# A chunked attention and feed-forward kernel: seven-product second layer from the third group of tokens on, its weight sums one group sooner

## The chip, the cores and the metric

The kernel runs on one core of a Trainium2 chip. Its time is in microseconds of the device, from the start to the end of one execution. A core has a matrix engine (TensorE, "PE" in the profile; its weight loads, "PEld", are listed apart), VectorE ("DVE"), ScalarE ("ACT"), GpSimd ("POOL") and SyncE ("SP"), which here issues nearly all transfers. The engines run their own instruction streams side by side and wait for one another by semaphores.

## The reference

```python
# q, k, v: (8, 8, 576, 64) fp32; w_in: (512, 2048), w_out: (2048, 512) fp32
q_c, k_c, v_c = (a.reshape(B, H, 9, 64, D) for a in (q, k, v))
scores = scale * np.matmul(q_c, k_c.transpose(0, 1, 2, 4, 3))     # scale = 1/8
scores = scores - np.max(scores, axis=-1, keepdims=True)
attn = np.exp(scores)
attn = attn / (np.sum(attn, axis=-1, keepdims=True) + 1e-09)
x = np.matmul(attn, v_c).reshape(B, H, S, D).transpose(0, 2, 1, 3).reshape(4608, 512)
h = x @ w_in
out = (h - np.tanh(h)) @ w_out
```

Attention is taken inside chunks of 64 tokens. Its result, 4608 tokens of 512, goes through a feed-forward net of two layers, with h − tanh(h) between them.

## The kernel before

**Tiles and groups.** The 4608 tokens are 36 tiles of 128, in nine groups of four (`SIZES`, L34), so 512 tokens a group. The hidden width of 2048 is cut into 16 units of 128, numbered fc. For each group and unit, the first layer makes the tile ph (128 hidden values by 512 tokens), ACT takes tanh of it, DVE subtracts (`shrink`, tile t), ACT rounds the result to a high half gh, DVE takes the low half gl = t − gh (`split`), and the second layer adds this unit's share to four output tiles po in PSUM. The second layer of a unit stands two units behind its first layer, and two ph tiles exist, so PE always has one layer to do while the others work on the unit between.

**Products of halves.** Every factor is held as a high and a low half, and a product is high x high, low x high and high x low, so three matmuls per block. In the plain form both layers of a unit take 3 x 4 = 12 matmuls of 128x512 (`gemm1`, L572, and `gemm2`, L601) on the 32-bit type F32R. From the third group (number 2) on the first layer uses 16-bit halves of the weights instead. In the fast form (`Fast`, L646) the unit is two 128-wide blocks of the hidden layer (j and j + 8) by two tiles of tokens, and the second layer is taken by seven products in place of eight, with sums and differences of blocks: 7 x 3 = 21 matmuls of 128x256 (L709). For it the weights need their own sums, once. `combine` (L499 to L523) makes them on POOL, five steps for each of eight j, and `shorten` (ACT L534, DVE L535) rounds four pieces of each to 16-bit halves. The activations need sums too, in each unit (POOL, L678 to L680).

**Weights.** They come as 64-bit words from two transfers a unit and are rebuilt on the chip: ACT L146, DVE L150, L151, L152 (shifts and masks that put the bits together), then the high half on ACT (`high`, L155) and the low half on DVE (`low`, L159). All of it lies in group 0. `square` (L110) gives ACT's sum of squares of a weight tile, from which powers of two for the 16-bit forms are made (`powers`, with `partition_all_reduce` on POOL). `convert` (L484 to L494) turns a first-layer weight tile into 16-bit halves: two operations on ACT (L490, L491), two on DVE (L493, L494).

**Which group does what, before.** Group 0 runs both layers in F32R. Its work follows `PLAN` (L55), a string of tokens; the part ahead of the bar is in exactly that order, the rest is placed by the scheduler. Group 1 too is F32R, from `run` (L603) with the scheduler's order; beside it lie the attention of group 2 (`interleaved`, L434), the squares of the second layer's weights and the 16 conversions. Group 2 has the 16-bit first layer, the second layer in F32R; it is written in a fixed order (`written`, L620, inside `manual_schedule`), and beside it lie the weight sums and their shortening, and attention of group 3. Groups 3 to 8 are the fast form, each beside the attention of the next group (`ahead`, L776). In the fixed order `at[k]` is a list of pieces that are issued at half step k: 2s after the first layer of the s-th unit, 2s + 1 after the second layer that follows it.

**Names.** wh and wl are the halves of a weight tile; a name like wl014 is layer 0, unit 14, and wh113 layer 1, unit 13. raw is a weight tile as loaded and w the rebuilt one. xh and xl are the halves of the token tiles, rawk and rawv the loaded keys and values of an attention, psa its PSUM tile, a and s its scores. gh and gl are the halves of the activations. place names that repeat a weight tile's name (wl11 as target of a sum) are other uses of the same memory.

Of the kernel before, what the change touches and what calls it, by code (L numbers as in the profile page):

```python
# [22 lines left out]
P = 128  # L23
H = 8
# [14 lines left out]
LAG = 2  # L39
FAST = 3  # L40
# [8 lines left out]


BASE = (3, 18)
LATER = (8, 20)
STEPS = (0, 1, 2, 3, 4, 5, 6, 11)
# [6 lines left out]
def attn_ffn_kernel(ctx: ExitStack, tc: tile.TileContext, qE, kE, vE, qL, kL, vL, w_in, w_out, out):  # L60
# [20 lines left out]
    wt, half_w, fast_w, w_pool = [[None, None] for _ in range(FC)], [None] * FC, {}, {}  # L81

# [29 lines left out]
    def power(pool, name, sums, to, back):  # L112


        n = sums.shape[1]
        top = pool.tile([P, n], F32, name=f"{name}top", bufs=2)
        nc.gpsimd.partition_all_reduce(top, sums, channels=P, reduce_op=bass_isa.ReduceOp.max)
        power_of_two(top, to, back)

# [5 lines left out]

    def largest(a, out):

        nc.vector.tensor_reduce(out=out, in_=a, axis=AX.X, op=ALU.max, apply_absolute_value=True)
        nc.vector.tensor_scalar_mul(out, out, 2.0 ** -12)
# [24 lines left out]
    def high(fc, part):  # L154
        nc.scalar.copy(out=wt[fc][part][0], in_=ws[fc][:, part].bitcast(F32))  # L155
# [118 lines left out]
    class Late:  # L274
# [4 lines left out]
        def __init__(self, pool):  # L279
            self.pool, self.st = pool, defaultdict(dict)  # L280

            self.raw = {n: xpool.tile([P, KC, MOST], F32R, name="xl").bitcast(F32) if n == "q" else pool.tile([P, MOST // P, H * CH], F32, name=f"raw{n}", bufs=1) for n in "qkv"}
            self.q16 = self.v16 = self.k16 = self.aT = self.junk = None

        def load(self, p, i):
            for n, src in (("q", qL), ("k", kL), ("v", vL)):
                nc.sync.dma_start(out=self.raw[n][:, i], in_=src[p - NE])

        def sums(self, g, n, other=None):
# [4 lines left out]
            some = self.raw[n][:, :SIZES[g]]  # L294
            if n != "v" and other is not None:
                spread(other.bitcast(U8).rearrange("p (a n) -> p a n", n=H * CH), some, d["sums"][:, "qkv".index(n):"qkv".index(n) + 1])
                return
            if n != "v":
                junk = self.pool.tile([P, 4, H * CH], F16, name="a", bufs=1).bitcast(U8).rearrange("p a n -> p (a n)")[:, :MOST * H * CH // P].rearrange("p (a n) -> p a n", n=H * CH) if self.junk is None else self.junk
                spread(junk, some, d["sums"][:, "qkv".index(n):"qkv".index(n) + 1])  # L300
                return
            largest(some.rearrange("p i n -> p (i n)"), d["sums"][:, 2:3])
            if other is None:
                self.scales(g)
# [10 lines left out]

        def scales(self, g):
            self.across(g)
            self.spread_out(g)
# [21 lines left out]
        def split(self, g, b, n):  # L340
# [4 lines left out]
            if n == "k":  # L345
                hl = self.k16
                if hl is None:
                    t = self.pool.tile([P, 2, 2 * H * CH], F16, name="a", bufs=1)
                    hl = t[:, 0], t[:, 1]
                d["k"] = hl  # L350
# [21 lines left out]
        def exponents(self, g, b):  # L372
            self.shifted(g, b)
            self.exponent(g, b)

# [11 lines left out]

        def normalise(self, g, b):
            self.totals(g, b)
            self.divided(g, b)  # L390
# [15 lines left out]
        def transpose(self, g, b):  # L406
# [5 lines left out]
            if self.aT:  # L412
                aT = self.aT
            else:
                t = self.pool.tile([P, 2, 4, 2, CH], F32, name="s", bufs=1).rearrange("p e hp c k -> p (e hp c k)").bitcast(F16)
                aT = [t[:, e * 2 * H * CH:(e + 1) * 2 * H * CH] for e in range(2)]
# [17 lines left out]
    def interleaved(att, g, x):  # L434

        at = defaultdict(list)
# [598 lines left out]
```

## Time and profile before

| What | us |
|---|---|
| Median of 3 runs | 820.54 |
| The runs | 818.73 to 821.04 |
| The profiled execution | 818.66 |
| Its span | 816.9 |
| PE busy | 803.5 |
| DVE busy | 644.5 |
| ACT busy | 467.4 |
| POOL busy | 381.1 |

The span is from the first to the last instruction; the profiled execution's own time is 1.8 us longer. Busy shares are averages over nine groups with different limits: group 0 has the weights to rebuild, groups 1 and 2 are single, groups 3 to 8 repeat. In a row of windows a stretch is given by its bounds in us, with the busy time of each engine and the number of its instructions. In the timeline a wait stands behind a row in brackets, with the instruction that ended it. Matmul rows overlap a little, since the next begins before the last has drained.

### The profile page before, as it was taken

The numbers are of one execution on the slowest core, as the hardware profiler recorded it, in microseconds if no ns is written. First come the engines' busy times: TensorE is split into PE (matmuls) and PEld (weight loads), VectorE is DVE, ScalarE is ACT, GpSimd is POOL, SyncE is SP. The second block draws the span as 40 slices with busy tenths as digits, with TensorE's granted clock in tenths as the row PEclk, the third lists the DMA queues.
The fourth block names the chain that finished last, engine by engine and source line by source line (L and its number), as shares of the span: only waits on it lengthen the run. The fifth ranks groups of instructions, "written<-read, shape, count | busy, mean of one in ns | idle before, by whom it ended". The sixth has DMA issues, their size and how long they took to land.

```text
span 816.9 us, 20560 instructions
## 1 busy us (share of the span) xinstructions
PE 803.5 (98%) x8805; PEld 664.6 (81%) x8805; DVE 644.5 (79%) x853; ACT 467.4 (57%) x754; POOL 381.1 (47%) x385
## 2 busy tenths in 40 slices
PE   8999999999999999999999999999999999999997
PEld 5677787788756568888888888888888888888886
DVE  6899986877459999797879787878887887877553
ACT  5698779665345457564745474546554655454332
POOL 2000000000028666856665756575666665757563
PEclk9999999999999999999999999999999999999999
DMA  7954523321201113122222322222222220202000
GB/s 250 344 180 156 187 86 140 105 53 34 71 1 30 49 37 120 27 79 53 80 53 79 53 79 53 79 53 79 52 80 52 79 53 2 53 3 52 2 27 26
DMA packets 58459, 63.19 MB, mean 77 GB/s; under 512 B 32768, under 2 KB 38912, under 8 KB 58368
## 3 DMA queue, kind: packets, MB, share of 16 engines
q1 hardware_dynamic: 57792, 61.10, 25.1%
q8 instruction: 69, 1.13, 0.6%
q10 hardware_dynamic: 576, 0.79, 0.3%
q14 instruction: 22, 0.18, 0.1%
HBM read 45.09 MB, written 9.44 MB: 67 GB/s over the span
## 4 chain that ended last, share of the span: by engine, by line
PE 80%; DVE 10%; ACT 5%; POOL 2%; issue 2%; DVEq 0%; ACTq 0%
PE ph L669 29%; PE po L709 26%; PE po L601 10%; PE ph L572 10%; PE psa L364 3%; PE ph L854 1%; DVE w L151 1%; DVE gl L592 1%; DVE w L152 1%; ACT wh L155 1%; ACT s L228 1%; ACT w L146 1%; ACT junk L110 1%; DVE wh L535 1%; PE psa L193 1%
## 5 line engine op out<-in xcount | busy, mean ns | idle before, releaser
L669 PE MATMUL ph<-xh,wl 128*128 128x256 f16 x2160 | 249.5, 273 | 0.0
L669 PEld LDWEIGHTS <-wl 128*128 128x128 f16 x2160 | 209.8, 98 | 25.2 <-issue 0.5
L678 POOL TENSOR_TENSOR xl<-xl 128x256 f32<-128x256 f32 x96 | 97.1, 1011 | 183.8 <-DVE xl L677 182.9
L676 ACT ACTIVATE t<-ph,sig 128x512 f32<-128x512 f32 x96 | 65.8, 685 | 147.6 <-PE ph L669 146.9
L677 DVE SCALAR_TENSOR_TENSOR xl<-ph,sig,t 128x512 f32<-128x512 f32 x96 | 71.6, 746 | 46.5 <-ACT t L676 46.3
L709 PEld LDWEIGHTS <-wh 128*128 128x128 f16 x1008 | 98.7, 98 | 11.4
L679 POOL TENSOR_TENSOR xl<-xl 128x128 f32<-128x128 f32 x96 | 105.5, 1099 | 0.0
L680 POOL TENSOR_TENSOR xl<-xl 128x256 f32<-128x256 f32 x96 | 93.1, 970 | 0.0
L709 PE MATMUL po<-wl,wh 128*128 128x256 f16 x576 | 89.7, 273 | 0.0
L690 DVE SCALAR_TENSOR_TENSOR wh<-xl,to_g,wh 128x896 f16<-128x896 f32 x48 | 64.6, 1346 | 30.0 <-ACT wh L689 30.0
L689 ACT ACTIVATE wh<-xl,to_g 128x896 f16<-128x896 f32 x48 | 49.9, 1039 | 60.8 <-POOL xl L680 60.8
L601 PE MATMUL po<-wh,gh 128*128 128x512 f32 x192 | 79.5, 414 | 1.0 <-ACT gh L591 0.8
L690 DVE SCALAR_TENSOR_TENSOR gl<-xl,to_g,gh 128x896 f16<-128x896 f32 x48 | 71.8, 1496 | 9.1 <-ACT gh L689 8.9
L601 PE MATMUL po<-wl,gh 128*128 128x512 f32 x192 | 75.7, 394 | 0.9 <-POOL wl L159 0.9
L572 PE MATMUL ph<-xh,wl 128*128 128x512 f16 (+2 forms) x316 | 76.5, 380 | 0.0
L601 PE MATMUL po<-wh,gl 128*128 128x512 f32 x192 | 75.1, 396 | 1.0 <-DVE gl L592 1.0
L709 PE MATMUL po<-wh,wh 128*128 128x256 f16 x432 | 75.9, 273 | 0.0
L709 PEld LDWEIGHTS <-gh 128*128 128x128 f16 x672 | 64.9, 98 | 7.8
L709 PE MATMUL po<-wh,gh 128*128 128x256 f16 x336 | 54.4, 273 | 0.0
L709 PE MATMUL po<-wl,gh 128*128 128x256 f16 x336 | 52.4, 273 | 0.0
L592 DVE TENSOR_TENSOR gl<-t,gh 128x512 fp32r<-128x512 f32 (+1 forms) x50 | 40.0, 800 | 15.5 <-ACT gh L591 15.3
L689 ACT ACTIVATE gh<-xl,to_g 128x896 f16<-128x896 f32 x48 | 49.5, 1032 | 4.2 <-POOL xl L680 4.1
(159 smaller groups left out, 1402.5 us busy)
## 6 DMA issues: line engine op xcount, KB each, us to landing
raw<-w_in SPq DMA_DIRECT2D x16, 512.0 KB, 3.7
raw<-w_out SPq DMA_DIRECT2D x16, 512.0 KB, 4.6
rawk<-kL SPq DMA_DIRECT2D x28, 256.0 KB, 3.9
rawv<-vL SPq DMA_DIRECT2D x28, 256.0 KB, 3.6
xl<-qL SPq DMA_DIRECT2D x28, 256.0 KB, 2.9
out<-wh SPq DMA_DIRECT2D x46, 128.0 KB, 1.8
q<-qE SPq DMA_DIRECT2D x8, 256.0 KB, 5.2
v<-vE SPq DMA_DIRECT2D x8, 256.0 KB, 4.5
```

The source lines that it names most:

```text
L572: nc.tensor.matmul(ph, lhsT=self.weight(fc, 0, a)[:, kc * P:(kc + 1) * P], rhs=x[b][:, kc, cols], start=(k == 0), stop=(k == 3 * KC - 1))
L592: nc.vector.tensor_sub(gl, t, gh)
L601: nc.tensor.matmul(self.po[t], lhsT=gg[a][:, ts], rhs=self.weight(fc, 1, b), start=(fc == 0 and i == 0), stop=(fc == FC - 1 and i == 2))
L669: nc.tensor.matmul(self.ph[:, 1 - f::2, :], lhsT=half_w[fc][:, w, kc * P:(kc + 1) * P], rhs=rhs, start=(k == 0), stop=(k == 3 * KC - 1))
L676: nc.scalar.activation(t, self.ph, AF.Tanh, scale=sig)
L677: nc.vector.scalar_tensor_tensor(out=u[:, :4], in0=self.ph, scalar=sig, in1=t, op0=ALU.mult, op1=ALU.subtract)
L678: nc.gpsimd.tensor_add(u[:, 4:6], u[:, 1:3], u[:, 0:4:3])
L679: nc.gpsimd.tensor_add(u[:, 6], u[:, 1], u[:, 2])
L680: nc.gpsimd.tensor_sub(u[:, 0:4:3], u[:, 0:2], u[:, 2:4])
L689: nc.scalar.activation(gh, u, AF.Copy, scale=powers[1])
L690: nc.vector.scalar_tensor_tensor(out=gl, in0=u, scalar=powers[1], in1=gh, op0=ALU.mult, op1=ALU.subtract)
L709: nc.tensor.matmul(place[m], lhsT=part[:, self.SUM[m]], rhs=w[m][:, o], start=first, stop=(last and part is gl), skip_group_check=True)
```

## The change

`FAST` goes from 3 to 2: the fast form, with its seven products, begins with the third group. For that, the weight sums and the 16-bit forms have to be there one group sooner.

- Group 1 is now written in a fixed order, over the units 0, 8, 1, 9 and so on (`ORDER`), as group 2 was. Beside it lie all that lay beside group 1 and group 2: powers of two, 16 conversions, sums of the second layer's weights for j from 0 to 5 and their shortening, and attention of group 2 (in place of that of group 3). The shortening of each j starts one step later than before, at 4j + 12 in place of 4j + 10; the sums start at the same half steps. The last two j follow at the start of group 2.
- `gemm2` in F32R takes for all four tiles first gh by wh and gh by wl, and then gl by wh for all four, in place of the three products tile by tile.
- The low half gl of the first four units of group 1 is made by POOL, the others by DVE.
- The high halves of first-layer weights of the units 8 to 15 (`SHORT`) are cut to 11 bits by a mask on DVE, into the memory of raw, before ACT copies them. With it the two DVE operations of `convert` are left out for these units.
- The measure of the second layer's weights is moved into group 0: for the first eight units squares on ACT, for the others (`SQUARED`) the largest absolute value by a reduction on DVE. `powers` is cut in two (`most`, with the reductions over the partitions, and `powers`).
- The loads for group 2's attention come as all of q, then k, then v.

```diff
-FAST = 3
+FAST = 2
+MASK = 0xFFFFE000
+SHORT = 8
+SQUARED = 8
+ORDER = tuple(i // 2 + i % 2 * FC // 2 for i in range(FC))
...
     def high(fc, part):
-        nc.scalar.copy(out=wt[fc][part][0], in_=ws[fc][:, part].bitcast(F32))
+        w = ws[fc][:, part]
+        if part == 0 and fc >= SHORT:
+
+            short = raws[fc][:, part].rearrange("p n a -> p (n a)")[:, :DM]
+            nc.vector.tensor_single_scalar(short, w, MASK, op=ALU.bitwise_and)
+            w = short
+        nc.scalar.copy(out=wt[fc][part][0], in_=w.bitcast(F32))
...
             nc.scalar.activation(l16, l, AF.Copy, scale=to)
+            if fc >= SHORT:
+                return
             rest = place_of("l", 0, fc)[:, :DM]
...
-    def split(self):
+    def split(self, engine=None):
...
-            nc.vector.tensor_sub(gl, t, gh)
+            (engine or nc.vector).tensor_sub(gl, t, gh)
...
-            for t in range(t0, t1):
-                ts = slice((t - t0) * P, (t - t0 + 1) * P)
-                for i, (a, b) in enumerate(((0, 0), (0, 1), (1, 0))):
-                    nc.tensor.matmul(self.po[t], lhsT=gg[a][:, ts], rhs=self.weight(fc, 1, b), start=(fc == 0 and i == 0), stop=(fc == FC - 1 and i == 2))
+            for some in ((0, 0), (0, 1)), ((1, 0),):
+                for t in range(t0, t1):
+                    ts = slice((t - t0) * P, (t - t0 + 1) * P)
+                    for a, b in some:
+                        nc.tensor.matmul(self.po[t], lhsT=gg[a][:, ts], rhs=wt[fc][1][b], start=(fc == 0 and a == b), stop=(fc == FC - 1 and a == 1))
...
             if self.ready:
-                self.split()
+                self.split(nc.gpsimd if s <= 4 else None)
...
     for fc in range(FC):
         square(fc, 0, junk)
+    for fc in range(SQUARED):
+        square(fc, 1, junk)
+    for fc in range(SQUARED, FC):
+        nc.vector.tensor_reduce(out=sums_w[1][:, fc:fc + 1], in_=wt[fc][1][0].bitcast(F32), axis=AX.X, op=ALU.max, apply_absolute_value=True)
...
+    at[0].append(loads)
+    at[1] += [lambda: half.most(0), lambda: half.most(1)]
+    at[4] += [lambda: half.powers(0), lambda: half.powers(1)]
+    for i, fc in enumerate(ORDER):
+        at[max(2 * i + 1, 5 + (3 * i + 1) // 2)].append(lambda i=i, fc=fc: half.convert(fc, place_of("l", 0, ORDER[i - 1]) if i else first_place))
...
     for j in range(FC // 2 - 2):
-        at[4 * j + 7].append(lambda j=j: make(j, 5))
+        at[4 * j + 7].append(lambda j=j: make(j, 5 if j else 4))
+        if j == 0:
+            at[11].append(lambda: make(0, 1))
         for i in range(4):
-            at[4 * j + 10 + i].append(lambda j=j, i=i: half.shorten(j, slice(i, i + 1)))
+            at[4 * j + 12 + i].append(lambda j=j, i=i: half.shorten(j, slice(i, i + 1)))
...
-        ff = FeedForward(FAST - 1, nx)
+        ff = FeedForward(1, nx)
...
-        for s in range(FC):
-            ff.written(s, s // 2 + s % 2 * FC // 2, at)
+        for s, fc in enumerate(ORDER):
+            ff.written(s, fc, at)
```

What this makes of the order is shown at three places. The first is DVE at the end of group 0, where the weights of the units 13 to 15 are rebuilt. Before, its rows were these (line, operation, target and sources, shape):

```order
L151 SCALAR_TENSOR_TENSOR w_1376<-raw_1373,w_1376 128x1024
L592 TENSOR_TENSOR gl_1358<-t_1354,gh_1357 128x512
L152 SCALAR_TENSOR_TENSOR w_1376<-raw_1373,w_1376 128x1024
L150 TENSOR_SCALAR w_1420<-w_1420 128x1024
L151 SCALAR_TENSOR_TENSOR w_1420<-raw_1417,w_1420 128x1024
L159 TENSOR_TENSOR wl014_1105<-w_1376,wh014_1104 128x512
L159 TENSOR_TENSOR wl114_1107<-w_1376,wh114_1106 128x512
```

Now, for the same unit 14 (its w is w_1382, its lines are some ten to fifteen lower):

```order
L847 TENSOR_REDUCE sums1_103<-wh112_1098 128x1
L137 SCALAR_TENSOR_TENSOR w_1382<-raw_1379,w_1382 128x1024
L136 TENSOR_SCALAR w_1427<-w_1427 128x1024
L138 SCALAR_TENSOR_TENSOR w_1382<-raw_1379,w_1382 128x1024
L527 TENSOR_TENSOR t_1405<-ph_1392,t_1405 128x512
L145 TENSOR_SCALAR raw_1379<-w_1382 128x512
L151 TENSOR_TENSOR wl114_1107<-w_1382,wh114_1106 128x512
L535 TENSOR_TENSOR gl_1409<-t_1405,gh_1408 128x512
L151 TENSOR_TENSOR wl014_1105<-w_1382,wh014_1104 128x512
```

A reduction (L847) and a mask (L145) stand between the operations of the unit, and its first-layer low half (wl014) now comes behind that of the second layer and behind a gl.

The second place is DVE in the middle of group 1. Before, between two subtractions t there stood a conversion (L493, L494) and at times a piece of attention (L354):

```order
L584 TENSOR_TENSOR t_2034<-ph_2021,t_2034 128x512
L354 SCALAR_TENSOR_TENSOR a_2235<-rawk_1543,to_1721,a_2235 128x1024
L592 TENSOR_TENSOR gl_2038<-t_2034,gh_2037 128x512
L493 SCALAR_TENSOR_TENSOR wl09_2197<-wh09_1084,to_w_1546,wl08_2194 128x512
L494 TENSOR_TENSOR wl08_2194<-wl08_2194,wl09_2197 128x512
L584 TENSOR_TENSOR t_2073<-ph_2060,t_2073 128x512
```

Now, in the eighth unit of the same group:

```order
L527 TENSOR_TENSOR t_1917<-ph_1904,t_1917 128x512
L447 SCALAR_TENSOR_TENSOR wl03_1923<-wh03_82,to_w_1570,wl010_1920 128x512
L448 TENSOR_TENSOR wl010_1920<-wl010_1920,wl03_1923 128x512
L330 SCALAR_TENSOR_TENSOR a_1926<-rawk_1567,to_1829,a_1926 128x1024
L489 SCALAR_TENSOR_TENSOR wh018_1839<-wh18_1741,to_w_1570,wh018_1839 128x512
L330 SCALAR_TENSOR_TENSOR wh09_1877<-rawv_1568,to_1829,wh01_1876 128x1024
L489 SCALAR_TENSOR_TENSOR wh02_1840<-wh10_1738,to_w_1570,wh02_1840 128x256
L535 TENSOR_TENSOR gl_1968<-t_1917,gh_1967 128x512
L527 TENSOR_TENSOR t_1984<-ph_1971,t_1984 128x512
```

Conversion, attention (L330) and two shortenings (L489) stand between one t and the gl that belongs to it.

The third place is PE, in the second layer of one unit of group 1. Before, the three products went tile by tile:

```order
L601 MATMUL po0_1568<-wh11_76,gh_1626 128x512
L601 MATMUL po0_1568<-wl11_77,gh_1626 128x512
L601 MATMUL po0_1568<-wh11_76,gl_1627 128x512
L601 MATMUL po1_1569<-wh11_76,gh_1626 128x512
L601 MATMUL po1_1569<-wl11_77,gh_1626 128x512
```

Now:

```order
L545 MATMUL po2_1577<-wl18_1083,gh_1645 128x512
L545 MATMUL po3_1578<-wh18_1082,gh_1645 128x512
L545 MATMUL po3_1578<-wl18_1083,gh_1645 128x512
L545 MATMUL po0_1575<-wh18_1082,gl_1646 128x512
L545 MATMUL po1_1576<-wh18_1082,gl_1646 128x512
```

The first matmul that reads gl moved from the third place of twelve to the ninth.

More of the change, by code (lines that the diff above doesn't have):

```diff
@@ L38 @@
 MOST = max(SIZES) * P
-LAG = 2
-FAST = 3
+FAST = 2
 FAST_LAG = 2
@@ L282, in __init__, with load, sums @@
             self.raw = {n: xpool.tile([P, KC, MOST], F32R, name="xl").bitcast(F32) if n == "q" else pool.tile([P, MOST // P, H * CH], F32, name=f"raw{n}", bufs=1) for n in "qkv"}
[L283 to L286 removed]
+            self.q16 = self.v16 = None
+        def load(self, p, i, some="qkv"):
+            for n in some:
+                src = {"q": qL, "k": kL, "v": vL}[n]
                 nc.sync.dma_start(out=self.raw[n][:, i], in_=src[p - NE])
[L289 removed]
+        def sums(self, g, n, other):
             d = self.st[f"g{g}"]
@@ L293, in sums @@
                 d["sums"] = self.pool.tile([P, 3], F32, name="sums", bufs=2)
[L294 to L304, printed above, removed]
+            spread(other.bitcast(U8).rearrange("p (a n) -> p a n", n=H * CH), self.raw[n], d["sums"][:, "qkv".index(n):"qkv".index(n) + 1])
         def halves(self, g, i):
@@ L411, in transpose @@
             nc.vector.tensor_sub(a[:, :, 1], s, a[:, :, 0])
[L412 to L416, printed above, removed]
+            t = self.pool.tile([P, 2, 4, 2, CH], F32, name="s", bufs=1).rearrange("p e hp c k -> p (e hp c k)").bitcast(F16)
+            aT = [t[:, e * 2 * H * CH:(e + 1) * 2 * H * CH] for e in range(2)]
             d["a16"] = []
@@ L553, in __init__ @@
             self.g, self.x, self.queue, self.po, self.ready = g, x, [], [], None
-            self.half = g > 1
-            if g > 1:
-                self.sig = half.power_of(g)[0]
-        def weight(self, fc, part, i):
-            return half_w[fc][:, i] if self.half and part == 0 else wt[fc][part][i]
         def room(self, pool, tiles):
@@ L571, in gemm1 @@
                 for kc in range(KC):
-                    nc.tensor.matmul(ph, lhsT=self.weight(fc, 0, a)[:, kc * P:(kc + 1) * P], rhs=x[b][:, kc, cols], start=(k == 0), stop=(k == 3 * KC - 1))
+                    nc.tensor.matmul(ph, lhsT=wt[fc][0][a][:, kc * P:(kc + 1) * P], rhs=x[b][:, kc, cols], start=(k == 0), stop=(k == 3 * KC - 1))
                     k += 1
@@ L781, in put @@
             at[o + 2 * unit + part].append(lambda: f(*args))
+        late = g == FAST
         for unit, n in (1, "q"), (2, "k"):
-            put(unit, 0, lambda n=n: att.sums(g, n, ffn.tile([P, MOST], F32, name="t", bufs=3)))
-        put(-3 if g > FAST else 1, 0, att.halves, g, 0)
-        put(2, 1, att.halves, g, 1)
+            put(unit + late, 0, lambda n=n: att.sums(g, n, ffn.tile([P, MOST], F32, name="t", bufs=3)))
+        put(3 if late else -3, 0, att.halves, g, 0)
+        put(3 if late else 2, 1, att.halves, g, 1)
         put(4, 1, att.across, g)
@@ L924, in attn_ffn_kernel, with loads @@
     late = ctx.enter_context(tc.tile_pool(name="att", bufs=1, side="right", reuse_waits="tile"))
+    w_pool.update((fc, late) for fc in SPARE)
     att, half = Late(late), Half(late)
[L926 to L929 removed]
+    xs, powers, at, made = {}, {}, defaultdict(list), {}
     first_place = late.tile([P, DM], F32, name="first_place", bufs=1).bitcast(F16)
[L931 to L957 removed]
+    def loads():
+        for n in "qkv":
+            for i in range(SIZES[FAST]):
+                att.load(FIRST[FAST] + i, i, n)
     def make(j, steps):
```

140 lines of the change are left out of this document (33 added, 107 removed).

## The prediction

> **What bounds the kernel now.** First the page: span, busy shares, and the chain that ended last, by engine.
>
> ```profile
> span 816.9 us, 20560 instructions
> PE 803.5 (98%) x8805; PEld 664.6 (81%) x8805; DVE 644.5 (79%) x853; ACT 467.4 (57%) x754; POOL 381.1 (47%) x385
> ...
> PE 80%; DVE 10%; ACT 5%; POOL 2%; issue 2%; DVEq 0%; ACTq 0%
> ```
>
> TensorE is busy for 98% of the span, so time is won by taking matmuls away and lost wherever another engine newly makes PE wait. Next the chain in order of time (start, us, engine, tile, line, count), from the end of group 0's weights to the first units of the seven-product groups.
>
> ```profile
> 92.28 2.35 DVE w L151 x2
> ...
> 168.33 2.76 PE ph L572 x12
> 171.09 2.80 PE po L601 x12
> ...
> 285.49 2.79 PE po L601 x12
> 288.28 2.60 PE ph L572 x12
> ...
> 354.19 2.62 PE ph L669 x24
> 356.81 2.29 PE po L709 x21
> ```
>
> Before 100 us the chain still runs through DVE (group 0's weights, L151); in the stages after it is PE. Then the windows of the stages touched (busy us of PE, PEld, DVE, ACT, POOL, granted clock, DMA share): the first has the stretch of group 2 in which the weight sums are shortened, then the end of group 0's weights, all of group 2, the start of group 3, and group 1.
>
> ```profile
> 247.30:300.40 53.10, 52.07 (x416) 32.32 (x415) 51.39 (x58) 26.48 (x41) 43.07 (x32) 1.00 0.15 41
> 100.00:120.00 20.00, 20.00 (x90) 16.57 (x89) 18.86 (x32) 14.51 (x31) 0.84 (x2) 1.00 0.34 110
> 220.80:305.30 84.50, 83.47 (x557) 51.32 (x557) 67.72 (x81) 42.62 (x65) 49.10 (x37) 1.00 0.12 37
> 311.10:350.90 39.80, 37.84 (x421) 32.76 (x423) 34.10 (x42) 25.49 (x34) 33.12 (x33) 1.00 0.25 68
> 128.00:220.80 92.80, 92.80 (x770) 74.66 (x768) 66.56 (x113) 59.33 (x96) 1.94 (x2) 1.00 0.21 61
> ```
>
> PE is full everywhere, at full clock. But DVE runs right behind it in two of the stages: 18.86 of 20 us at the end of group 0, and 51.39 of 53.10 us where the weight sums are made. Group 1 is easy: DVE 66.56 of 92.80, POOL idle. The change lays work on DVE in the first and moves the crowd of the second into group 1.
>
> **What is taken away.** Group 2's second layer goes from twelve 128x512 matmuls per unit to 21 of 128x256: 2.79 us (row 285.49) to 2.29 (356.81), 16 units: −8.0 us. Its first layer becomes 24 half-width matmuls, 2.62 against 2.60: +0.3. Sum **−7.7 us**, on PE, which sets the end there. Group 1's own matmuls stay as many (other order only).
>
> **The end of group 0.** On DVE come eight masks (L145 of the changed kernel, 128x512) and eight largest-value reductions (L847). The nearest rows of DVE's timeline (start, us of one or of x, line, tiles): a reduction over 128x512, a bit operation on 128x1024, the last weights, and two operations right behind each other.
>
> ```profile
> 70.01 0.68 DVE L237 TENSOR_REDUCE sm<-s 128x8 f32<-128x512 f32 x1
> ...
> 100.43 0.69 DVE L150 TENSOR_SCALAR w<-w 128x1024 uint32<-128x1024 uint32 x1
> ...
> 115.55 1.29 DVE L159 TENSOR_TENSOR wl<-w,wh 128x512 fp32r<-128x512 f32 x2
> ...
> 304.65 0.68 DVE L592 TENSOR_TENSOR gl<-t,gh 128x512 fp32r<-128x512 f32 x1
> 305.25 0.74 DVE L581 SCALAR_TENSOR_TENSOR t<-ph,sig,t 128x512 f32<-128x512 f32 x1
> ```
>
> PE's timeline: the first layer of group 0's last unit, and its last wait there.
>
> ```profile
> 118.51 1.07 PE L572 MATMUL ph<-xh,wh 128*128 128x512 f32 x4
> 119.41 1.07 PE L572 MATMUL ph<-xh,wl 128*128 128x512 f32 x4
> ...
> 124.82 0.50 PE L601 MATMUL po<-wh,gh 128*128 128x512 f32 x1 [0.23 <-ACT gh L591]
> ```
>
> An operation of 0.68 holds the engine for about 0.60 (rows 304.65 and 305.25: the next starts 0.60 later). A mask of half the row at 100.43 is so worth 0.33, and 8 x 0.33 = 2.6; six of the eight reductions stand ahead of the last low half by the order of the changed kernel, 6 x 0.60 = 3.6. Together 6.2 us of new work on an engine with 1.1 idle in 20. The cover: the last low weight half is done at 116.84, PE first uses it at 119.41, 2.6 later. In the new order three second-layer matmuls of 0.23 stand ahead of that first layer, and the wait of 0.23 at 124.82 can go, together about 1.0. So 6.2 − 2.6 − 1.0 = **+2.5 us**, rounded; the ends are 0 (DVE's idle time and ACT, rid of half the squares in group 1, take it) and 6.2 (no cover).
>
> **Group 1 as the crowded stage.** What squeezed group 2 was shortening on DVE beside POOL's sums. Groups by form in group 2's stage (busy, mean ns of one, idle before):
>
> ```profile
> L592 DVE TENSOR_TENSOR gl<-t,gh 128x512 fp32r<-128x512 f32 x15 | 17.0, 1132 | 3.1 <-ACT gh L591 3.1
> ...
> L535 DVE SCALAR_TENSOR_TENSOR wl<-wh,to_w,wl 128x512 f16<-128x512 f32 x10 | 9.6, 960 | 0.0
> ```
>
> All this now stands in group 1, and with it part of the conversion of the first layer's weights, which used to lie in group 1 alone. The groups there:
>
> ```profile
> L493 DVE SCALAR_TENSOR_TENSOR wl<-wh,to_w,wl 128x512 f16<-128x512 f32 x15 | 11.2, 748 | 4.8 <-PE ph L572 3.4 <-ACT wl L491 1.4
> ...
> L494 DVE TENSOR_TENSOR wl<-wl,wl 128x512 f16<-128x512 f16 x15 | 6.3, 422 | 0.3
> ```
>
> The conversions of the masked eight need no DVE any more. Of the other eight, five fall into the steps in which sums are shortened, two shortenings a step as before. Alone they cost 5 x (0.748 + 0.422) = 5.9 us; stretched like the shortenings, which are operations of the same kind (0.960 against 0.748, 1.28 times), 7.5; stretched like gl (1.132 against 0.68, 1.66 times), 9.7. Ten steps of group 1 (2.76 + 2.80 = 5.56 against 2.79 + 2.60 = 5.39) are 1.7 longer. So DVE has 4.2 to 8.0 us more to do than that stage allowed before; by the kind that is nearest, 5.8.
>
> How far may it fall behind? ACT's tanh, and rows of PE's timeline: the only wait on gl, the last unit's first layer, and the wait after the stage.
>
> ```profile
> 303.83 0.69 ACT L580 ACTIVATE t<-ph,sig 128x512 f32<-128x512 f32 x1
> ```
>
> ```profile
> 280.32 0.50 PE L601 MATMUL po<-wh,gl 128*128 128x512 f32 x1 [1.03 <-DVE gl L592]
> ...
> 299.89 2.76 PE L572 MATMUL ph<-xh,wl 128*128 128x512 f16 x12
> 302.31 0.58 PE L601 MATMUL po<-wh,gh 128*128 128x512 f32 x1
> ...
> 350.86 0.94 PE L364 MATMUL psa<-a,wh 64*64 64x64 f16 x92 [1.94 <-DVE a L354]
> ```
>
> There are two ph buffers: the first layer of unit n+2 begins two units after that of unit n began, 2 x 5.39, and that of unit n itself takes 302.31 − 299.89 = 2.42 up to the next matmul. In the 8.36 between must lie tanh (0.69) and the subtraction (0.74): 6.9 us are left. The last unit's products end at 302.65 (299.89 + 2.76), tanh could be done 0.69 later, and DVE starts the subtraction at 305.25: it was 1.9 behind at the end of the stage. That leaves 5.0. The low half gl is now first needed by the ninth matmul of a unit instead of the third, 6 x 0.23 = 1.4 later: 6.4 in reserve against 5.8, so on balance nothing is lost. But the wait of 1.03 at 280.32 came with the reserve far from used up: single low halves stand behind a bunch of attention work. The new stage has two bunches with conversions in them, steps 7 and 8 and step 14. I give each the middle of the two waits that DVE's bunches caused before (1.03 and 1.94), 1.5, and take off the 1.03 of the stage that is replaced: **+2.0 us**. The ends: −1.0, all covered, since the first four units' low halves go to POOL (idle there: 1.94 of 92.80) and the ninth matmul waits less; and 8.0, if no lag can be carried. I take 2.0, because it comes from waits on the same engine in the stage most like it. I count on the lag carried out of the stage being made up in the next one, where DVE has 39.80 − 34.10 = 5.7 us free.
>
> At nothing go: POOL's gl, about 1.4 us each (the POOL rows below) with more than one whole first layer, 2.76, before it is needed, which would cost its length if that cover went; the two reductions over the partitions and the small powers, early in group 1 where DVE has 28% free; the loads of group 2 in another order, at least two steps ahead of their use; the mask's ACT cast, which is as long as before.
>
> **The sum.** −7.7 + 2.5 + 2.0 = −3.2 us. The profiled run took 818.66 us (span 816.9), 1.88 below the median of the runs, 820.54. So 815.5 in that run and **817.3** against the median.
>
> [...] Beside POOL the same subtraction differs widely; a row of DVE's timeline, then two of POOL's from the same stretch:
>
> ```profile
> 257.13 1.78 DVE L592 TENSOR_TENSOR gl<-t,gh 128x512 fp32r<-128x512 f32 x1
> ```
>
> ```profile
> 257.00 1.36 POOL L509 TENSOR_TENSOR wh<-wh,wl 128x512 f32<-128x512 f32 x1
> 258.44 1.61 POOL L512 TENSOR_TENSOR wl<-wh,wh 128x512 f32<-128x512 f32 x1
> ```
>
> 1.78 us beside POOL and 0.68 alone (304.65): the mean of 1.13 in this stage is a blend. [...]
>
> **The rivals.** The forecast above (A) has both costs partly covered: **817.3**, chance 0.34.
> B, both covers hold: DVE's additions at the end of group 0 fall into gaps and lag that PE never sees, and the crowd costs no more than the 1.03 it cost before; −7.7 + 0.7 (one late weight, the 0.23 of 124.82 three times) = −7.0, **813.5**. For it: in the crowded stage PE lost 1.0 us in 84.5. Against it: 1.1 us of idle time in 20 for 6.2 of work. 0.28.
> C, the lag goes on into group 2: of the 5.8 us, 1.0 shows in group 1 and the other 4.8 at the start of group 2, where DVE begins the seven-product units behind. Before, such a lag of 1.9 was followed by a wait of 1.94 on DVE's attention work at 350.86. +4.8 on A's −3.2 = +1.6, **822.1**. Against it are the 5.7 us that DVE has free there. 0.22.
> [...] 0.16.
> That the change does not do what it says is ruled out by its order: group 2's units hold 21 matmuls.
>
> **How the numbers follow.** A measurement of this kernel tells about 0.3% from no change, 2.5 us: faster is below 818.1, slower above 823.0. A gives 0.25 faster and 0.09 same; B 0.28 faster; C 0.15 same and 0.07 slower; D 0.03 same and 0.13 slower: 0.53, 0.27, 0.20. The range reaches from B's 813.5 less 1.0 of scatter, 812.5, over C to 824.5, which leaves out most of D (0.12) and a bit below B (0.06).
>
> **What would show it.** Right: second-layer rows of 2.3 us from the third group on; group 0's last unit beginning about 2.5 us late, with PE waits on ACT's or DVE's weights between 95 and 125 us; waits of PE on gl or ph in group 1's second half, 3 us in all; none over 2 us in group 2's start. Wrong: no PE wait in group 1 (B), waits over 4 us after it (C), or waits on DVE at unit after unit of group 1 (D).

## The result, and the profile after

The changed kernel takes 834.0 us (median of 4 runs, 832.42 to 834.41) against 820.67 (median of 4 runs, 818.73 to 821.04): 1.0164 times as long, 95% interval 1.0143 to 1.0185. So it is slower by 13.3 us, and the forecast was 817.3 us, faster. The profiled execution took 834.25 us.

The page of the changed kernel: span, busy shares, and the chain that ended last, by engine.

```profile
span 832.5 us, 21288 instructions
PE 803.1 (96%) x9141; PEld 683.4 (82%) x9141; DVE 660.4 (79%) x858; ACT 471.5 (57%) x742; POOL 436.7 (52%) x443
...
PE 77%; DVE 12%; ACT 5%; issue 3%; POOL 2%; DMA 0%; DVEq 0%; SPq 0%; ACTq 0%
```

PE is busy 803.1 us, as long as before (803.5), though it has 7.7 us less to do. It also stands still for 832.5 − 803.1 = 29.4 us, 16.0 more than before. The waits of PE tell where (engine, tile, line, who ended the wait: us in total, times, longest):

```profile
PE po L545 <- POOL gl L535: 6.1, 1, 6.1
PE psa L340 <- DVE a L330: 4.6, 3, 1.9
PE po L545 <- ACT gh L534: 3.2, 5, 1.1
PE po L545 <- DVE gl L535: 2.4, 2, 2.0
PE ph L595 <- DVE xl L603: 2.1, 1, 2.1
...
PE psa L340 <- DVE from L113: 0.8, 1, 0.8
PE psa L340 <- ACT a L329: 0.5, 1, 0.5
```

The longest is a single one of 6.06 us, on a low half gl that POOL makes. The same in windows of 40 us (PE, PEld, DVE, ACT, POOL busy, granted clock, DMA share): end of group 0, group 1, its passage to group 2, group 2.

```profile
100.00:140.00 40.00, 37.68 (x160) 29.28 (x159) 30.38 (x52) 24.91 (x51) 1.17 (x3) 1.00 0.42 141
140.00:180.00 40.00, 33.94 (x138) 26.88 (x137) 19.53 (x36) 22.17 (x34) 17.77 (x15) 0.91 0.05 15
180.00:220.00 40.00, 36.46 (x246) 28.58 (x245) 39.59 (x47) 25.32 (x41) 28.12 (x22) 1.00 0.18 47
220.00:260.00 40.00, 35.70 (x425) 29.60 (x424) 36.67 (x45) 27.52 (x41) 23.96 (x23) 1.00 0.20 67
260.00:300.00 40.00, 37.31 (x498) 32.38 (x496) 34.04 (x49) 22.51 (x32) 28.08 (x29) 0.96 0.22 54
300.00:340.00 40.00, 39.97 (x540) 35.50 (x539) 31.83 (x33) 23.16 (x29) 25.49 (x27) 1.00 0.25 68
```

PE loses time in each of the first five, and in two of them its clock falls as well. In 140 to 180 no engine that PE waits for is near full: DVE works 19.53 of 40 us. In 180 to 220 DVE is full. From 300 on PE is full, as before. POOL's timeline at the start of group 1 shows what PE waited for at 147.54.

```profile
137.60 0.38 POOL L420 PARTITION_ALL_REDUCE top<-most  x1 [106.87 <-DMA out<-t]
137.90 0.52 POOL L423 PARTITION_ALL_REDUCE whole<-sums  x1
138.37 0.41 POOL L420 PARTITION_ALL_REDUCE top<-most  x1
146.24 2.50 POOL L535 TENSOR_TENSOR gl<-t,gh 128x512 fp32r<-128x512 f32 x2 [7.47 <-issue]
```

Between the last reduction over the partitions and the first subtraction POOL stood still for 7.47 us and waited for nothing that the profile shows ("issue"). In the order in which the kernel gives POOL its instructions a row stands at this place that the forecast passed over:

```order
...
16 L420 ISA top_1623<-most_1617 128x1
17 L535 ISA
18 L535 TENSOR_TENSOR gl<-t,gh 128x512 x3
```

Row 17 has no operands. It stands between the last reduction and the first ordinary operation. In the trace it shows as two short rows of POOL's sequencer (POOLq), of 84 ns each:

```profile
L535 POOLq MODIFY_POOL_CONFIG  x2: 84/84/84, 138.7 to 138.7; - x2
```

In the kernel before the same row stood ahead of the first weight sum (L506) and ran at 148.1, while POOL had nothing else to do for 47.69 us:

```profile
147.64 0.52 POOL L117 PARTITION_ALL_REDUCE w1top<-most  x1 [28.29 <-DVE undo_g L542]
195.85 1.43 POOL L506 TENSOR_TENSOR wh<-wh,wl 128x512 f32<-128x512 f32 x1 [47.69 <-DVE wl L493]
```

The PE rows around the wait show a second loss:

```profile
147.54 2.08 PE L545 MATMUL po<-wh,gl 128*128 128x512 f32 x4 [6.06 <-POOL gl L535]
149.41 1.91 PE L519 MATMUL ph<-xh,wh 128*128 128x512 f32 x4
151.12 1.88 PE L519 MATMUL ph<-xh,wl 128*128 128x512 f32 x4
152.83 1.10 PE L519 MATMUL ph<-xl,wh 128*128 128x512 f32 x4
```

Four matmuls take 1.9 to 2.1 us in place of 1.1 until 152.8: the granted clock from 147.5 to 152.8 is 0.50, so PE runs at half its clock behind the wait.

What the forecast had right stands further on. In the chain in order of time, the third group now has the units of the fast form, 2.62 and 2.29 us:

```profile
286.43 2.62 PE ph L595 x24
289.05 2.29 PE po L635 x21
```

### The profile page after: what moved, and what is told of

It is laid out like the page before. It is cut to its first block, busy times and chain, and to the rows that moved or that the text cites. A ratio compares the mean times of both kernels' runs of the same rounds, so it can differ in the third digit from the quotient of the medians.

```text
span 832.5 us, 21288 instructions
## 1 busy us (share of the span) xinstructions
PE 803.1 (96%) x9141; PEld 683.4 (82%) x9141; DVE 660.4 (79%) x858; ACT 471.5 (57%) x742; POOL 436.7 (52%) x443
## 3 DMA queue, kind: packets, MB, share of 16 engines
q8 instruction: 71, 1.16, 0.6%
## 4 chain that ended last, share of the span: by engine, by line
PE 77%; DVE 12%; ACT 5%; issue 3%; POOL 2%; DMA 0%; DVEq 0%; SPq 0%; ACTq 0%
PE ph L595 33%; PE po L635 30%; PE ph L519 4%; PE po L545 4%; PE psa L340 3%; DVE wh L489 1%; PE ph L779 1%; DVE gl L535 1%; DVE t L527 1%; DVE w L138 1%; DVE wl L489 1%; ACT s L220 1%; ACT wh L147 1%; DVE w L137 1%; DVE w L136 1%
## 5 line engine op out<-in xcount | busy, mean ns | idle before, releaser
L595 PE MATMUL ph<-xh,wl 128*128 128x256 f16 x2520 | 291.3, 273 | 2.1 <-DVE xl L603 2.1
L595 PEld LDWEIGHTS <-wl 128*128 128x128 f16 x2520 | 244.9, 98 | 31.6 <-issue 2.8
L604 POOL TENSOR_TENSOR xl<-xl 128x256 f32<-128x256 f32 x112 | 111.7, 997 | 217.0 <-DVE xl L603 216.4
L635 PEld LDWEIGHTS <-wh 128*128 128x128 f16 x1176 | 115.1, 98 | 13.3
L603 DVE SCALAR_TENSOR_TENSOR xl<-ph,sig,t 128x512 f32<-128x512 f32 x112 | 83.5, 746 | 52.5 <-ACT t L602 52.2
L605 POOL TENSOR_TENSOR xl<-xl 128x128 f32<-128x128 f32 x112 | 124.5, 1112 | 0.0
L606 POOL TENSOR_TENSOR xl<-xl 128x256 f32<-128x256 f32 x112 | 108.2, 966 | 0.0
L635 PE MATMUL po<-wl,wh 128*128 128x256 f16 x672 | 104.6, 273 | 0.0
L545 PE MATMUL po<-wh,gh 128*128 128x512 f32 x128 | 52.2, 408 | 3.4 <-ACT gh L534 3.2
L545 PE MATMUL po<-wl,gh 128*128 128x512 f32 x128 | 50.7, 396 | 0.9 <-POOL wl L151 0.9
L545 PE MATMUL po<-wh,gl 128*128 128x512 f32 x128 | 37.0, 406 | 8.5 <-POOL gl L535 6.1
L635 PEld LDWEIGHTS <-gl 128*128 128x128 f16 x392 | 38.6, 99 | 4.7
```

Source lines behind the costliest of these rows:

```text
L545: nc.tensor.matmul(self.po[t], lhsT=gg[a][:, ts], rhs=wt[fc][1][b], start=(fc == 0 and a == b), stop=(fc == FC - 1 and a == 1))
L595: nc.tensor.matmul(self.ph[:, 1 - f::2, :], lhsT=half_w[fc][:, w, kc * P:(kc + 1) * P], rhs=rhs, start=(k == 0), stop=(k == 3 * KC - 1))
L603: nc.vector.scalar_tensor_tensor(out=u[:, :4], in0=self.ph, scalar=sig, in1=t, op0=ALU.mult, op1=ALU.subtract)
L604: nc.gpsimd.tensor_add(u[:, 4:6], u[:, 1:3], u[:, 0:4:3])
L605: nc.gpsimd.tensor_add(u[:, 6], u[:, 1], u[:, 2])
L606: nc.gpsimd.tensor_sub(u[:, 0:4:3], u[:, 0:2], u[:, 2:4])
```

## The experiments

The theory after the result was: T, POOL's change from the reductions to ordinary operations takes some 7.5 us, and the low halves queued behind it stop PE; B, the additions on DVE at the end of group 0 cost what their waits show; C, the rest is DVE behind in group 1 and at the passage to group 2, by the conversions. The rivals are in the expectations; the letters there are their own, and B, C and D are not the rivals B, C and D of the prediction. The times, against runs of the kernel before on the same chip (818.8 to 819.1 in the median; 820.67 for the changed kernel):

| Kernel | Median, us | Ratio to before, 95% |
|---|---|---|
| changed kernel | 834.0 | 1.0143 to 1.0185 |
| gl_dve | 824.17 | 1.0034 to 1.0080 |
| gl_pool_late | 823.8 | 1.0028 to 1.0065 |
| no_allreduce | 823.47 | 1.0041 to 1.0074 |
| squares_act | 821.49 | 1.0017 to 1.0036 |
| no_convert_dve | 817.44 | 0.9964 to 0.9985 |
| old_order | 822.42 | 1.0030 to 1.0053 |
| short_early | 823.06 | 1.0024 to 1.0057 |
| mask_none | 827.78 | 1.0092 to 1.0120 |
| mask_all | 817.91 | 0.9971 to 0.9993 |
| measure_late | 816.84 | 0.9961 to 0.9979 |
| mask_all_early | 818.86 | 0.9986 to 1.0006 |
| measure_late_early | 817.76 | 0.9975 to 0.9993 |
| across_late | 818.87 | 0.9979 to 0.9997 |
| act_late | 815.78 | 0.9943 to 0.9967 |

**POOL's change-over: gl_dve, gl_pool_late, no_allreduce.** Each starts from the changed kernel. The first two differ in who makes gl in group 1:

```diff
-                self.split(nc.gpsimd if s <= 4 else None)
+                self.split()                                       # gl_dve
+                self.split(nc.gpsimd if s in (3, 4) else None)     # gl_pool_late
```

> All low halves gl of group 1 on DVE, none on POOL; nothing else changed. Theory T (POOL stands still for about 7.5 us between the last reduction over the partitions and its first ordinary operation, and the low halves of the first units are queued behind that): the wait of 6.06 us at 147.54 goes, and with it the half clock behind it (about 2.4 us), so about 8.5 us less than the changed kernel, near 825.5. Rival U (the 6 us come from the start of group 1 as such, from tanh, loads or the powers of two, and another engine is late next): less than 3 us gained, 831 or more.

> POOL makes the low halves of the third and fourth unit only, DVE those of the first two. Theory T: POOL is ready again before it is asked for the third unit, so the gain is the same as with no low half on POOL, 8.5 us, near 825.5, within 1.5 us of it. Rival W (an ordinary low half on POOL is too slow or shut out by DVE, 1.28 us or more against 0.68, so each of the four costs): about half of the 8.5 us stays, near 829.5.

The third keeps POOL's low halves and takes away what comes ahead of them:

```diff
-            nc.gpsimd.partition_all_reduce(top, most, channels=P, reduce_op=bass_isa.ReduceOp.max)
+            nc.gpsimd.tensor_copy(top, most)
...
-                nc.gpsimd.partition_all_reduce(self.whole, q, channels=P, reduce_op=bass_isa.ReduceOp.add)
+                nc.gpsimd.tensor_copy(self.whole, q)
```

> The changed kernel with POOL's low halves as they are, but the three reductions over the partitions replaced by plain copies on POOL, so the powers of two are taken per partition and not over all (a part left out). Theory T (POOL's 7.5 us come from changing over from the reductions to ordinary operations): the row ahead of the first low half is gone from POOL's order, the wait of 6.06 us on it goes, and the time falls by about 9.8 us, as with no low half on POOL, to near 824. Rival W (low halves on POOL are late by themselves): the wait stays above 3 us, 830 or more.

Measured: 824.17, 823.8 and 823.47 us, so 9.8 to 10.5 us less, three ways. POOL in gl_dve:

```profile
137.75 0.73 POOL L420 PARTITION_ALL_REDUCE top<-most  x1
145.96 1.29 POOL L460 TENSOR_TENSOR wh<-wh,wl 128x512 f32<-128x512 f32 x1 [7.48 <-ACT t L526]
```

and in no_allreduce, where the operand-less row between the two is gone from POOL's order:

```profile
138.33 0.18 POOL L420 COPY top<-most 128x1 f32<-128x1 f32 x1 [0.48 <-DVE most L418]
138.47 2.54 POOL L535 TENSOR_TENSOR gl<-t,gh 128x512 fp32r<-128x512 f32 x2
```

The pause is there in gl_dve too, 7.48 us, but nobody waits for POOL then; in gl_pool_late it is 6.93. Without the reductions the low halves follow at once, and made by POOL, in 1.27 to 1.30 us each, they keep PE waiting nowhere. The reductions themselves follow one another within 0.5 us (137.60, 137.90, 138.37 in the changed kernel), so the pause belongs to what comes between them and the ordinary operations. T holds, U and W fall: POOL's operations were not too slow, they stood behind a change-over. No operation fills the pause: in the changed kernel the two MODIFY_POOL_CONFIG rows of 84 ns stand at 138.7 and the first low half at 146.24. It was 6.93 (gl_pool_late), 7.47 (the changed kernel) and 7.48 us (gl_dve), each time between the last reduction and the first ordinary operation.

**The end of group 0: squares_act.** From gl_dve:

```diff
-SQUARED = 8
+SQUARED = 16
```

> All low halves on DVE, and the measure of all 16 second-layer weights as squares on ACT in group 0, so the eight reductions of DVE are gone. Theory B (the additions on DVE at the end of group 0 cost what the waits of 0.51, 1.06 and 1.05 on gh there show, 2.6 us in all): about 2 us less than with all low halves on DVE, if the eight further squares on ACT (about 0.75 us each, 6 us) find room before group 1's first tanh; with them in the way, up to 4 us more. Rival C (the end of group 0 costs nothing, the crowd in group 1 all of it): no gain at the end of group 0, waits on gh there unchanged.

Measured 821.49, 2.7 us less than gl_dve. The three waits of PE on gh in gl_dve, at 91.08, 103.65 and 116.22 (0.52, 1.07 and 1.07 us), are gone but for one of 0.19; the squares filled ACT's gaps between 119.8 and 134.2 and kept no one waiting. B holds.

**The crowd: no_convert_dve, mask_none, old_order, short_early.** The first is from gl_dve, the others from squares_act.

```diff
-            if fc >= SHORT:
-                return
+            return                                     # no_convert_dve
...
-SHORT = 8
+SHORT = 16                                             # mask_none
...
-            for some in ((0, 0), (0, 1)), ((1, 0),):   # old_order: as before the change
-                for t in range(t0, t1):
+            for t in range(t0, t1):
+                for i, (a, b) in enumerate(((0, 0), (0, 1), (1, 0))):
...
-            at[4 * j + 12 + i].append(lambda j=j, i=i: half.shorten(j, slice(i, i + 1)))
+            at[4 * j + (10 if j else 12) + i].append(lambda j=j, i=i: half.shorten(j, slice(i, i + 1)))   # short_early
```

> All low halves on DVE, and the two DVE operations of the conversion left out for all 16 units, so the low-order part of eight first-layer weights is not added: this prices the conversions on DVE. Theory C (the crowd of group 1 is the loss that is left, by the eight conversions of 1.17 us): the waits on gl (0.37 and 2.00) and those at the passage to group 2 (1.64, 2.13, 0.76, 1.94 and the half clock behind the last) shrink by 4 us or more against all low halves on DVE, near 821. Rival D (these waits come from attention and shortening alone, whatever the conversions): less than 1.5 us gained.

> All low halves on DVE, all squares on ACT, no mask, so all 16 conversions take DVE. Theory C in numbers: from 16 to 8 masked cost 821.5 − 817.9 = 3.6 us net; if each conversion on DVE costs the same, none masked costs 3.6 more, near 825. If PE's waits grow out of proportion once DVE is behind (queue already full, half clock behind each wait), 828 or more. If the first eight masks gain nothing, 821.5.

> All low halves on DVE, all squares on ACT, and the second layer of groups 0 and 1 tile by tile as before the change, so gl is needed by the third matmul. Forecast's step (gl needed 1.4 us later is worth 1.4 us at each place where PE waits on gl): the waits on gl in group 1 grow from 0.4 and 2.0 to 1.8 and 3.4, near 824.3, more if the clock falls behind a wait. Rival F (a late gl only delays work that is then late by the next wait anyway): less than 1 us slower.

> All low halves on DVE, all squares on ACT, and the shortening of the sums j = 1 to 5 one step earlier, where it was before the change. Theory L (the shortening one step later pushes DVE's lag into the start of group 2, the waits of 2.13 and about 1 us there): these waits shrink by 1 to 2 us, near 820. Rival P (POOL's sums are not ready that early, so DVE waits for POOL with tanh's subtraction queued behind it): new waits of PE in group 1, 822 or more.

Measured: 817.44 without the conversions on DVE, 6.7 less than gl_dve; 827.78 with all 16, 6.3 more than squares_act, more than the 3.6 that a straight line gave and just short of 828. So eight conversions, 9.4 us of DVE alone (8 x 1.17), cost 6 to 7 us of the time: C's size holds, D falls. The place is not where C had it. In gl_dve PE waits 1.04, 0.36 and 2.00 us in group 1 and 0.73, 2.13 and 1.11 at the passage (splits of the attention, L330, and in the middle the subtraction). Without the conversions those of group 1 are gone, and those of the passage stay: 0.38 and 1.16 on the split, 2.25 on the subtraction. One of two stretches of half clock goes too. So the conversions cost in group 1; the passage has other causes (below).

The order of the second layer's products hardly matters: old_order is 0.9 us slower than squares_act in the median, with runs that overlap (820.87 to 823.77 against 820.76 to 822.79), not the 2.8 expected. F holds. The waits on gl were then 1.53, 0.32 and 2.03, against 0.38 and 2.00: a new one came, and the other two did not grow.

Shortening earlier, as before the change, costs 1.6 us in the median (823.06 against 821.49; the runs overlap, 820.68 to 824.56). The wait of 2.13 at the passage is gone, but the lag comes out elsewhere:

```profile
PE psa L340 <- DVE a L330: 4.3, 3, 1.9
PE po L545 <- DVE gl L535: 2.7, 1, 2.7
PE psa L340 <- ACT a L329: 1.9, 1, 1.9
```

L was right on the wait and wrong on the time: with DVE full, moving one piece of its work moves the wait. P's mechanism had a small part at most: ACT waited once, 1.5 us, for a sum of POOL's, and DVE never.

**A mask on all units: mask_all, mask_all_early.** From squares_act, so that no conversion needs DVE; the second with the shortening earlier, as in short_early.

```diff
-SHORT = 8
+SHORT = 0
```

> All low halves on DVE, all squares on ACT, and the mask on the first-layer weights of all 16 units in place of eight, so that no conversion needs DVE. Theory C (conversions on DVE in the crowd cost the 6.7 us that leaving them out gained): 821.5 less 6 to 7, with eight masks of 0.33 more on DVE in group 0, which is full up to 100 us, 2.6 at most: 815 to 818, faster than before by 0.1 to 0.5%. Rival E (the added masks lengthen group 0 by more than their own time, since they stand ahead of ACT's high half in the first units): 819 or more.

> As with all 16 masked, and the shortening of j = 1 to 5 one step earlier, where it was before the change. Theory R (with no conversion left on DVE there is room for the shortening in group 1, and the wait of 2.26 at the start of group 2 goes as it did with eight masked, without the waits of 2.69 and 1.88 that took its place there): 2 to 4 us gained, near 815. Rival P (attention's splits and scores are late behind the shortening whatever the conversions): no gain or a loss, 818 or more.

mask_all measures 817.91, 3.6 us less than squares_act and faster than the kernel before (0.9971 to 0.9993). The eight further masks cost one wait of 2.0 us early in group 0 (PE on ACT's high half, L147); in group 1 all waits on gl are gone. Shortening earlier again gives nothing (818.86). The wait of 2.26 is gone, as R had it, but waits of 0.85 on gh, 1.47 on gl and 1.93 on the split stand elsewhere: P.

**The passage to group 2: measure_late, measure_late_early, act_late, across_late.** In mask_all the longest wait left was 2.26 us on the subtraction L603 at 235.70. ACT and DVE ahead of it:

```profile
228.02 1.89 ACT L106 ACTIVATE t<-xl 128x2048 uint8<-128x2048 f32 x1
...
229.91 0.71 ACT L488 ACTIVATE wl<-wh,to_w 128x512 f16<-128x512 f32 x1
```

```profile
230.65 0.92 DVE L489 SCALAR_TENSOR_TENSOR wl<-wh,to_w,wl 128x512 f16<-128x512 f32 x1 [1.32 <-ACT wl L488]
...
234.90 0.74 DVE L603 SCALAR_TENSOR_TENSOR xl<-ph,sig,t 128x512 f32<-128x512 f32 x1
```

ACT's sum over the elements for group 3's queries (L106) stands ahead of the high half of a shortening (L488), DVE waits 1.32 us for that, and the subtraction that frees ph stands behind it on DVE. The variants move group 3's measures; act_late only ACT's part:

```diff
-            put(unit + late, 0, lambda n=n: att.sums(g, n, ffn.tile([P, MOST], F32, name="t", bufs=3)))
+            put(unit + (g <= FAST + 1), 0, lambda n=n: att.sums(g, n, ffn.tile([P, MOST], F32, name="t", bufs=3)))   # act_late
...
+        next_one = g == FAST + 1                       # measure_late: as act_late, and
-        put(3 if late else -3, 0, att.halves, g, 0)
-        put(3 if late else 2, 1, att.halves, g, 1)
+        put(3, 0, att.halves, g, 0) if late else put(2, 1, att.halves, g, 0) if next_one else put(-3, 0, att.halves, g, 0)
+        put(3 if late or next_one else 2, 1, att.halves, g, 1)
...
-        put(4, 1, att.across, g)                       # across_late: as measure_late, and
-        put(5, 1, att.spread_out, g)
+        put(5 if next_one else 4, 1, att.across, g)
+        put(*((6, 0) if next_one else (5, 1)), att.spread_out, g)
```

> As with all 16 masked (all low halves on DVE, all squares on ACT), and group 3's measures of q, k and v one unit later at the start of group 2 (ACT's two sums over the elements, 1.9 us each, and DVE's two largest values, 1.21 each; one of these leaves the end of group 1). Theory S (the wait of 2.26 on the subtraction at 235.70, with about 2 us of half clock behind it, comes from ACT's sum of 1.89 at 228.02, behind which DVE waits 1.32 for its next shortening): the wait shrinks by 1.3 or more and the half clock goes, 2 to 4 us gained on the kernel with all 16 masked, near 815. Rival Q (DVE's own queue there, copies and sums of attention, sets it): less than 1 us gained, 817 or more.

> Both: all 16 masked, group 3's measures one unit later and the shortening one step earlier. If theories S and R both hold, the two share one wait, so it gains no more than 1 us over the better of the two, near 814. If P holds, it is no better than the later measures alone.

> As with all 16 masked, and of group 3's measures only ACT's two sums one unit later; DVE's largest values stay where they were. Theory S alone (ACT's sum at 228.02 keeps DVE's next shortening waiting for 1.32 us): the wait of 2.26 at 235.70 shrinks by about 1.3 and no wait of 2.3 on the measures takes its place, as it did with all measures later; without the half clock that followed, 1.3 to 3.3 us gained on the kernel with all 16 masked, 814.5 to 816.5. Rival Q (DVE's queue sets it): less than 0.7 gained.

> As with all of group 3's measures one unit later, and also the transposition that collects them and the powers of two made from it one unit or half a unit later. Theory G (the wait of 2.30 on the measures cost twice: itself and the half clock of about 4 us behind it, 2 us): with the wait gone, 3 to 4.5 us gained on the 816.8 with the measures later, near 813. Rival H (the half clock is not tied to the wait, only the wait itself counts): 2 us gained, near 814.8. Rival J (the next step, the split of group 3's queries, is late in its place): less than 1 us gained.

act_late measures 815.78 us, 2.1 less than mask_all, and is the fastest version found: 0.9943 to 0.9967 of the kernel before. Its wait at that place is 1.17:

```profile
236.28 2.78 PE L595 MATMUL ph<-xh,wl 128*128 128x256 f16 x24 [1.17 <-DVE xl L603]
243.93 0.27 PE L303 MATMUL psa<-ident,sums 128*3 128x128 f32 x1 [0.28 <-ACT t L106]
...
265.48 0.94 PE L340 MATMUL psa<-a,wh 64*64 64x64 f16 x92 [1.94 <-DVE a L330]
```

S holds for this wait, against Q: 1.1 us of it go with ACT's sum. That the whole gain of 2.1 comes from there is not shown. The wait at 265.48 is 1.94 here and was 1.09 in mask_all, and the two profiled spans are 814.9 and 814.2, the other way round; the gain stands between the medians (runs from 815.31 to 816.65 against 816.01 to 819.28). With DVE's measures moved too (measure_late, 816.84) the same 1.1 us is won on the wait, and PE waits 2.30 us for the transposition of those measures. across_late moves that transposition, and PE then waits 3.68 us at the next step, a second small matmul (L312) for a maximum that DVE takes too late (818.87). That is J in kind, though the late step is this matmul and not the split of the queries, so the time could not separate G from H. (The last section has what the traces show of the half clock behind such waits.) With the shortening earlier (measure_late_early, 817.76) nothing is gained.

## Why the prediction was wrong

**The gain on PE was right.** The third group's units take 2.62 + 2.29 us, as counted: −7.7.

**The end of group 0 was right in size, not in place.** Forecast +2.5; the waits are 0.51, 1.06 and 1.05 us, 2.6, and taking the reductions off DVE gained 2.7. Operations started 0.33 us behind a mask and 0.59 or 0.60 behind a reduction, as counted. But the forecast measured the cover at the last low half of a weight, in group 0's last unit. PE waited in three units, from 91 us on, for ACT's gh: that stood on ACT behind the high half of a weight, which waited 1.2 to 1.3 us for DVE to rebuild the weight (L138). That the sum met the measured 2.6 so closely is in part luck.

**The step that failed: "At nothing go: POOL's gl, ... with more than one whole first layer, 2.76, before it is needed, ... the two reductions over the partitions".** Each of them was cheap and covered by itself. What was left out is what lies between them: POOL's change from one to the other, 6.93 to 7.48 us, more than the 2.76 of cover. It had an entry in POOL's order and was hidden in the trace of before by 47.69 us of idle time. It cost 9.8 to 10.5 us between the medians, by three experiments. In the traces that is 6.06 of waiting and some 2.6 of half clock (5.3 us at half, up to 152.8), 8.7 together, and the profiled spans of the changed kernel and no_allreduce differ by 8.9 (832.5 and 823.6). Without it the changed kernel would be at 824, in the forecast's range and still not faster.

**The crowd was too small in the sum.** The forecast gave +2.0 and chose rival C's mechanism as the less likely. Group 1 itself was right: waits of 1.05, 0.37 and 2.00, less the 1.03 of the stage replaced, are 2.4. But then waits stood at the passage to group 2, where C had them: 0.52, 1.64, 2.13, 0.76 and 1.94 us, 7.0, less the 1.94 that stood there before, 5.1; C had 4.8. The failed sentence is "I count on the lag carried out of the stage being made up in the next one, where DVE has 5.7 us free". The free time is an average over 40 us, and these waits come at single places in them.

That C's 4.8 is so near the 5.1 is luck, for C had the lag come from the crowd of conversions. The 2.13 on the subtraction stays at 2.25 without any conversion on DVE (no_convert_dve) and falls from 2.26 to 1.17 when ACT's sum of 1.89 no longer stands ahead of a shortening, behind which the subtraction that frees ph has to wait (mask_all, act_late). The splits' waits are smaller as soon as DVE makes the low halves (0.73 and 1.11 in gl_dve); why, no run shows. Behind the last of the waits the clock fell too, to 0.50 for 3.41 us.

The parts make −7.7 + 2.6 + 10 + 2.4 + 5.1 = +12.4, with the half clock of 1.7 from 282.5 on some 14; measured were 13.3 between the medians and 15.6 between the two profiled spans.

**How long DVE's operations take beside POOL's sums** did not decide it. Among its crowd gl took 1129 ns in the mean, against 1132 before, and a conversion's two operations 932 and 821 ns in place of 748 and 422: 1.75 us each, where the forecast took 1.50 and its upper end, stretched like gl, 1.94. What lengthens them no run shows. The groups of the changed kernel from 165 to 240 us:

```profile
L535 DVE TENSOR_TENSOR gl<-t,gh 128x512 fp32r<-128x512 f32 x11 | 12.4, 1129 | 0.0
...
L447 DVE SCALAR_TENSOR_TENSOR wl<-wh,to_w,wl 128x512 f16<-128x512 f32 x6 | 5.6, 932 | 2.4 <-ACT wl L443 2.4
L448 DVE TENSOR_TENSOR wl<-wl,wl 128x512 f16<-128x512 f16 x6 | 4.9, 821 | 0.2
```

Neither of rival B's two covers held. D, the slower case at 0.16, had the right sign, but PE's waits for DVE of more than 0.2 us stood at three places of group 1 (1.05 us at 183.44, 0.37 at 203.76, 2.00 at 211.63), not at unit after unit.

**Gain that the change could have had.** With the low halves on DVE, the squares on ACT, all units masked and ACT's sums one unit later, the same seven-product group gives 815.78: 3.3 us of the 7.7 are kept, and the waits at 236.28 and 265.48 show where some of the rest went.

## What to carry to other kernels

Work that is moved to an idle engine is not free because the engine is idle: look at what stands directly ahead of it in that engine's order, also at rows without operands, and ask whether the trace of before hid their time in an idle stretch. A lag is made up where its first waiter stands, not over the mean of the next stage: follow the queue of each engine to the one operation that frees the buffer. Where an engine is full, moving one piece of its work moved the wait (short_early, measure_late, across_late), and taking work off it shortened the time (here a mask of 0.42 us in place of a conversion of 1.75).

## What the runs showed of the hardware that was not expected

A wait of PE can cost more than itself. The same wait of 2.00 us on the same gl was followed by half clock in one kernel and by full clock in the next. First gl_dve, where the wait ends at 202.2, then the changed kernel, where it ends at 211.6 (windows with the busy time of PE first, the granted clock third from the end):

```profile
198.99:202.41 3.42, 1.43 (x7) 0.85 (x6) 3.42 (x3) 1.62 (x3) 3.34 (x3) 1.00 0.00 0
202.41:205.82 3.41, 3.41 (x9) 2.63 (x9) 3.41 (x4) 2.95 (x5) 3.21 (x3) 0.50 0.18 34
205.82:209.23 3.41, 3.41 (x17) 2.80 (x16) 3.38 (x6) 2.50 (x4) 1.39 (x1) 1.00 0.65 122
```

```profile
207.45:210.87 3.42, 2.19 (x10) 1.43 (x8) 3.42 (x3) 1.73 (x3) 3.26 (x3) 1.00 0.00 0
210.87:214.28 3.41, 2.65 (x12) 2.17 (x12) 3.41 (x4) 2.01 (x4) 3.41 (x4) 1.00 0.00 0
214.28:217.69 3.41, 3.41 (x17) 2.82 (x16) 3.41 (x6) 2.73 (x6) 1.19 (x2) 1.00 0.83 154
```

Seventeen matmul pieces pass in 3.41 us with the clock at 1.00, nine at 0.50. The windows are not chosen around the wait. In the clock records of each trace every stretch of half clock inside the run lasts 3.41 us, or twice that, and the stretches of one trace begin whole multiples of 3.41 us apart (146.01 and 282.54 in the changed kernel, 202.41 and 243.37 in gl_dve), wherever the waits lie. So in these traces time is cut by a grid of 3.41 us, whose place differs from trace to trace, and the windows above lie on it. In gl_dve all of the wait falls into one window, 2.0 us without PE, and the next window has half clock. In the changed kernel the grid cuts it into 1.2 and 0.8, and nothing follows. The wait of 1.94 at 281.43 in the changed kernel lies in one window (279.13 to 282.54), with half clock behind it; that of 1.94 at 350.86 in the kernel before is cut by the grid at 350.00, and the clock stays at 1.00.

Counted over all 16 traces, without their first 5 us and what comes after 800: all 24 full-clock windows in which PE stood still for 1.9 us or more were followed by half clock, three of the five with 1.79 to 1.89, and none of the others, which have 1.72 or less. PE need not stand still throughout such a window: in gl_dve it worked 1.43 us of 198.99 to 202.41, and the next window had 0.50. A stretch of 3.41 us at half is worth up to 1.7 us of PE (an estimate, half its length). So in these traces a wait of about 2 us cost up to 1.7 us more where most of it fell into one window, and behind full-clock windows with 1.72 us or less without PE the clock stayed.
